# Splitting a bankful of projections over two bursts, and starting a block's projections twelve pairs past its flip

## The chip, the cores and the metric

The kernel runs on one core of one Trainium2 chip. The metric is the device time of one launch in microseconds (us); the median of the runs before is 2676.86 us. The engines are TensorE (PE, with its weight loads listed as PEld), VectorE (DVE), ScalarE (ACT), GpSimd (POOL), and SyncE (SP), which issues most of the DMAs. PE writes its results to PSUM, which has eight banks; one bank holds 128 x 512 float32 values.

## The reference, cut to what matters

Two layers of two kinds alternate, A B A B, over a sequence of S = 2048 tokens with D = 576 features, 32 heads of 18 features each. A is attention with one shared head of keys and values, B is linear attention with a feature map of two softmaxes:

```python
# A: x + A(layernorm(x)); 32 query heads, one key and one value head
q = (x @ wq).reshape(B, S, H, Dh).transpose(0, 2, 1, 3)
k, v = x @ wk, x @ wv
p = softmax(einsum("bhqd,bkd->bhqk", q, k) * Dh ** -0.5)
o = einsum("bhqk,bkd->bhqd", p, v).reshape(B, S, H * Dh) @ wo

# B: x + B(layernorm(x)); linear attention
q, k, v = split(x @ wqkv)
pq, pk = q @ w_phi, k @ w_phi                          # per head
phi = concatenate([softmax(p), softmax(-p)])           # for pq and for pk
kv, z = einsum("bhsf,bhsd->bhfd", phi_k, v), phi_k.sum(s)
o = (phi_q @ kv) / (phi_q @ z + 1e-6) @ wo
```

## The kernel before, in words

The attention of A is the long part of the kernel, a loop that is run once in each of the two A/B layers, in `attend`. It goes over 16 blocks of 128 tokens (`c`), each in two groups of 16 heads (`g`), and for each group over the 16 key tiles (`t`). One (`c`, `g`, `t`, half of the heads) is a *pair*: two score matmuls of 512 columns that run side by side on the two halves of PE's rows (L574), written to one `sc` tile of two banks, and one exponential of 1024 columns on ACT (L1047) that reads `sc` and writes a `pt` tile. There are three `sc` tiles, so the scores of a pair need the exponential three pairs earlier to be done. Two pairs of a key tile make one *value step*: eight matmul records (L853, float32 in two passes) that add probabilities times values to the group's accumulator, one PSUM bank. A layer has 1024 pairs and 512 value steps, and 64 pairs go to one block of tokens.

The six score banks leave two banks. They are called `ps` and `acc`: one of them is the accumulator of the running group, the other is the spare bank for all other PE work. When a group opens (its value step `t == 0`), `homes.reverse()` swaps the two: the spare bank becomes the new accumulator.

The other PE work of the loop is the projections of A's output and of layer B. They run for one block of 128 tokens after the other, as PE has room between scores and values. A *bankful* is one 128 x 288 result: 14 matmuls (L257), because each float32 product is made of a high and a low part. A block of tokens takes eight bankfuls: two of the output projection (weights `wd`, named `wdhi` and `wdlo` in the profile), then two of keys (`wa`), two of values (`wb`) and two of B's queries (`wc`), and then 32 small matmuls that update B's state (L651, the *update*, stored by `kv`). When a bankful is complete DVE copies it out of the spare bank (L607 for keys and queries, L638 for values, L321 for the output). For keys and queries DVE then makes minima, maxima and differences (L609 to L612) and ACT takes an exponential (L614). Ahead of the second query bankful, DVE normalises the first (`feature_end`: L619 to L621).

When a group closes, DVE turns its accumulator (`turned`, L955), divides it by its sums, turns it back (`osb`) and splits it in high and low parts (L134, L135). `tick()` issues the next piece of that work, up to twice in a burst.

The order on PE and on DVE is written by the program and pinned with `in_order()`. `burst()` writes it: three pairs of scores; then a bankful if the `credit`, which grows by the pace of 0.39 in each burst, has reached 1, if the burst before had none and if enough `pt` tiles are free; otherwise two value steps, or three when the next burst will have a bankful, and the update if it is its turn. When the projections have nothing to do (`idle`), the loop goes in steps of two pairs and one value step.

`stream()` decides which projection work comes next. A block that has its attention output added is *flipped*: normalised on DVE and turned through DRAM (`flip_tokens`, `fetch_tokens`), then split in high and low parts on DVE (`turn_tokens`, `split_tokens`), and then its keys, values and queries begin (`mix`) once `wanted()` says so. Before, that is when the attention of the next block has closed, or when fewer than 100 pairs are left.

Of the kernel before, what the change touches and what calls it, by code (L numbers as in the profile page):

```python
# [19 lines left out]
P = 128  # L20
# [4 lines left out]
NT = S // P  # L25
# [3 lines left out]
NG = 2  # L29
# [33 lines left out]
def kernel(ctx, tc, x_in, wq, wk, wv, wo, wqkv, w_phi, wob, out):  # L63
# [264 lines left out]
    def fold_phi(ps, pool, slow, more, folded):  # L328
# [35 lines left out]
        def turn():  # L364
# [12 lines left out]
            for _ in range(2):  # L377
                yield STAGE
# [548 lines left out]
    def attend(layer, st, a1o, stream):  # L927
# [13 lines left out]
        with ctx1:  # L941
# [65 lines left out]
            kind, credit, paused = [None], [0.0], [False]  # L1007
# [12 lines left out]
            def fill():  # L1020
                kind[0] = None
                while True:
                    v = next(bulk[0])
                    assert v is not STAGE
                    if v < 0:
                        break
                in_order()
# [68 lines left out]
            def sums(until):  # L1096
                while done[0] < until:
                    n, t, _ = units[2 * done[0]]
                    values(*groups[n], t, [pts.pop((n, t, hh)) for hh in range(2)])
                    done[0] += 1  # L1100
                    in_order()
# [4 lines left out]
            def burst():  # L1106
# [5 lines left out]
                if work == "P" and credit[0] >= 1 and not paused[0] and held <= TILES:  # L1112
                    fill()
                    credit[0] -= 1
                    paused[0] = True
                else:
                    paused[0] = False
                    count = 3 if credit[0] + st["pace"] >= 1 else 2
                    until = min(ready, max(done[0] + count, -(-(at[0] + BURST - TILES) // 2)))
                    opens = any(t % NT == 0 for t in range(done[0], until))  # L1120
                    if work == "F" and credit[0] >= 1 and not opens:
                        fill()
                        credit[0] -= 1
                        until = min(until, max(done[0] + 1, -(-(at[0] + BURST - TILES) // 2)))
# [23 lines left out]
    BURST = 3  # L1148
    TILES = 9
# [3 lines left out]
    PACES = ((0.6, 0.39), (0.39, 0.39))  # L1153
    FLIP = 84
    TAIL = 100
# [123 lines left out]
    for layer in range(LAYERS):  # L1279
        last = layer == LAYERS - 1  # L1280
        st.update(start_state(bw), added=set(), loaded=set())
        with tc.tile_pool(name="a1o", bufs=2) as a1o:
# [12 lines left out]
            def stream(v, layer=layer):  # L1295
# [58 lines left out]
                settled = 0  # L1354

                def turn_tokens():
                    nonlocal xs, fetched, settled
                    if fetched is not None:
# [4 lines left out]
                def wanted():  # L1363
                    return (xs is not None and xs[0] != KEPT and v.left() <= settled
                            and (xs[0] < st["closed"] or xs[0] == NT - 2 or v.left() < TAIL))

                def flip(i, stats):
                    nonlocal fetched
# [3 lines left out]
                    fetched = i, fetch_tokens(i)  # L1372
# [24 lines left out]
                while v.left():  # L1397
                    if finished:
                        yield from finish_tile()
                    elif turning and xs is None:  # L1400
# [3 lines left out]
                        yield from rest(8)  # L1404
                        turn_tokens()
                    elif fetched is not None and xs is None:
                        yield from rest(8)
                        turn_tokens()
                    elif fetched is None and xs is None and unflipped and v.left() > FLIP:
# [7 lines left out]
                        yield from rest(8)  # L1417
                        turn_tokens()
# [158 lines left out]
```

## Time and profile before

| | |
|---|---|
| runs | 2676.86 us median of 3 (2673.14 to 2677.76) |
| the profiled execution's own time | 2676.42 us |
| its span, first to last instruction | 2674.6 us |
| mean granted TensorE clock | 0.991 of full speed |
| PE busy | 2602.2 us, 97% |
| ACT busy | 2153.8 us, 81% |
| DVE busy | 1265.0 us, 47% |
| ACT idle before the loop's exponentials | 180.4 us, of it 160.3 us waiting for scores |

The loop of the first layer fills the time from about 111 to 1216 us of the span, that of the second from about 1449 to 2525 us. Ahead of, between and behind them lie the first projections of queries, B's read-out and the weights of the next layer, which the change leaves as they are. The ends of matmuls in the profile are modelled, and PE shows as busy nearly everywhere in the loops; how fast the loop runs is better read from the starts of its score matmuls. In the rows below the columns of a timeline are: start in us, length in us, engine, line, operation, result and operands, shapes, number of instructions merged, and in brackets the idle time before it and what ended it.

### The profile page before, as it was taken

The page shows a single profiled execution, that of the slowest core. Times are in us where ns is not written, and L with a number is a line of the kernel's source. Part 1 is how long each engine was busy: PE and PEld are TensorE (multiplying, and loading weights), DVE is VectorE, ACT ScalarE, POOL GpSimd, SP SyncE. Part 2 cuts the span into 40 slices and gives each one's busy share as a digit, 9 for nine tenths or more (in the row PEclk, how much of TensorE's full clock was granted, in tenths as well). Part 3 has the DMA queues.
Part 4 walks back from the last instruction along what each step waited for, and adds up shares of the span by engine and source line. Part 5 has one row for each costly group of instructions (what it writes and reads, how often), then busy time and mean ns, then how long its engine had stood idle before and what let it go on. Part 6 is the DMA issues. An engine that isn't in the chain of part 4 may idle for free. (4 is left out here: it accounts for less than half of the span.)

```text
span 2674.6 us, 55524 instructions
## 1 busy us (share of the span) xinstructions
PE 2602.2 (97%) x22002; PEld 1442.2 (54%) x22002; DVE 1265.0 (47%) x2871; ACT 2153.8 (81%) x2529; POOL 66.0 (2%) x106
## 2 busy tenths in 40 slices
PE   7989999999999999999999999999999999999999
PEld 6633454445444444438996344444444444444498
DVE  8435354444444444436774424444444444444265
ACT  4588889989999999994334999999999999999821
POOL 1000000000000000002000000000000000000010
PEclk9999999999999999999999999999999999999999
DMA  5466243222222222225643312222222222222164
GB/s 182 144 146 171 70 127 100 59 53 60 60 59 57 55 57 57 59 66 158 188 152 105 105 51 59 60 60 60 59 60 59 60 60 57 56 55 55 48 196 140
DMA packets 491634, 232.97 MB, mean 87 GB/s; under 512 B 237734, under 2 KB 458214, under 8 KB 491366
## 3 DMA queue, kind: packets, MB, share of 16 engines
q1 hardware_dynamic: 489894, 226.37, 31.4%
q8 instruction: 177, 2.90, 0.5%
q10 hardware_dynamic: 1472, 2.95, 0.4%
q14 instruction: 91, 0.75, 0.1%
HBM read 130.62 MB, written 96.67 MB: 85 GB/s over the span
## 5 line engine op out<-in xcount | busy, mean ns | idle before, releaser
L1047 ACT ACTIVATE pt<-sc 128x1024 f32<-128x1024 f32 x2036 | 1923.4, 1054 | 180.4 <-PE sc L574 160.3
L574 PE MATMUL sc<-qst,kst 56*128 56x512 f32 x3840 | 698.6, 452 | 21.0 <-ACT pt L1047 20.6
L574 PEld LDWEIGHTS sc<-qst,kst 56*128 56x128 f32 x3840 | 319.4, 185 | 561.7 <-ACT pt L1047 511.8
L853 PE MATMUL acc<-pt,vst 128*32 128x512 f32 x4096 | 499.8, 600 | 0.1
L853 PE MATMUL ps<-pt,vst 128*32 128x512 f32 x4048 | 486.7, 604 | 6.1 <-DVE featq L607 3.2
L853 PEld LDWEIGHTS ps<-pt,vst 128*32 128x32 f32 x4048 | 109.8, 110 | 234.0 <-issue 226.1
L853 PEld LDWEIGHTS acc<-pt,vst 128*32 128x32 f32 x4096 | 104.6, 109 | 211.7 <-issue 209.2
L321 DVE TENSOR_TENSOR xc<-xc,acc 128x288 f32<-128x288 f32 x60 | 27.3, 455 | 349.5 <-PE acc L257 349.5
L257 PE MATMUL ps<-wahi,xs 128*128 128x288 f32 x702 | 152.5, 304 | 2.5 <-ACT xs L132 1.9
L257 PE MATMUL ps<-wchi,xs 128*128 128x288 f32 x576 | 127.2, 307 | 0.0
L257 PE MATMUL acc<-wdhi,on 128*128 128x288 f32 x540 | 120.6, 309 | 3.3 <-DMA on<-od 3.3
L257 PEld LDWEIGHTS ps<-wahi,xs 128*128 128x128 f32 x702 | 116.1, 190 | 7.1 <-ACT xs L132 2.6
L257 PE MATMUL ps<-walo,xs 128*128 128x288 f32 x390 | 114.9, 297 | 0.0
L452 PE MATMUL ps<-xsc,wbhi 128*128 128x256 f32 x576 | 107.3, 285 | 0.6 <-ACT xsc L132 0.6
L474 ACT ACTIVATE pc<-ps 128x256 fp32r<-128x256 f32 x80 | 30.4, 384 | 94.0 <-PE ps L452 92.5
L257 PEld LDWEIGHTS ps<-wchi,xs 128*128 128x128 f32 x576 | 94.1, 188 | 19.0 <-issue 18.1
L607 DVE COPY featk<-acc 128x288 f32<-128x288 f32 x50 | 22.8, 457 | 172.0 <-PE acc L257 172.0
L132 ACT ACTIVATE xs<-ps 128x512 fp32r<-128x512 f32 x36 | 21.4, 595 | 102.6 <-PE ps L307 102.6
L257 PEld LDWEIGHTS acc<-wdhi,on 128*128 128x128 f32 x540 | 88.8, 189 | 25.0 <-issue 23.6
L257 PE MATMUL acc<-wahi,xs 128*128 128x288 f32 x450 | 100.0, 308 | 0.5
L257 PE MATMUL ps<-wclo,xs 128*128 128x288 f32 x320 | 94.3, 295 | 0.0
L452 PEld LDWEIGHTS ps<-xsc,wbhi 128*128 128x128 f32 x576 | 91.2, 192 | 1.6 <-ACT xsc L132 1.1
(261 smaller groups left out, 3062.3 us busy)
## 6 DMA issues: line engine op xcount, KB each, us to landing
qst<-qd SPq DMA_DIRECT2D x360, 72.0 KB
od<-parts SPq DMA_DIRECT2D x512, 36.0 KB
pht<-phi SPq DMA_DIRECT2D x32, 540.0 KB
qd<-pc SPq DMA_DIRECT2D x64, 256.0 KB
on<-od SPq DMA_DIRECT2D x60, 256.0 KB
phi<-pht SPq DMA_DIRECT2D x104, 144.0 KB
xd<-xc SPq DMA_DIRECT2D x33, 288.0 KB
flipped<-pht SPq DMA_DIRECT2D x112, 72.0 KB
```

The costliest lines, as they stand in the source:

```text
L132: A.activation(dst_hi, src, AF.Copy)
L257: T.matmul(dst, xs[:, slot, :], w[half][:, k, c0 : c0 + HALF], start=(n == 0), stop=(n == last))
L321: V.tensor_add(xr, xr, po)
L452: T.matmul(po, lhs, xsc[:, slot, :], start=(n == 0), stop=(n == LASTP))
L474: A.activation(pc[:, 0, :], po, AF.Copy)
L574: T.matmul(sc, kst[head_rows(h), t * P : (t + 1) * P], q[head_rows(h), h // 2, :], start=True, stop=True)
L607: V.tensor_copy(e[:, hs, 0, :], src)
L853: T.matmul(acc[32 * j : 32 * j + 32, :], vst[:, t, :], pts[j], start=first, stop=last)
L1047: A.activation(pt, sc, AF.Exp, scale=SCALE)
```

## The change

Three things are changed in the loop; nothing of what is computed changes.

1. A bankful may be written in two parts. In a burst that follows one without projections, with half a credit, the new branch writes one value step, then the first `PIECE` steps of the bankful (6 of its 14 matmuls); in a later burst it writes one value step and the other 8. Each part takes half a credit. A bankful that can go whole (a full credit, enough free `pt` tiles) still does, as before with no value step beside it. A part is not begun where a group opens within the next six value steps; a group that opens while a bankful is parted has its rest written first. The pace falls from 0.39 to 0.38.
2. `mix` of block `i` may begin when the loop is two pairs short of the end of block `i + 1`, whether that block is closed or not (`BLOCK`, `EARLY`); the rule with `TAIL` goes.
3. The split of a flipped block (`turn_tokens`) waits for `RIPE` = 12 pairs since its flip, instead of eight ticks; finished blocks go first.

In the folding of the weights of the first layer, one load now also waits for a free buffer before it is issued.

```diff
--- before.py
+++ after.py
@@ -375,6 +375,8 @@
                     ready[0] = n - 2
                     yield STAGE
             for _ in range(2):
+                yield STAGE
+            while len(units) - done[0] > len(wts):
                 yield STAGE
             load(len(units) - 1)
             for n in range(2):
@@ -1004,7 +1006,7 @@
                                 tc.add_manual_dep(i, last[PE], SYNC if loads_at[0] is None else NOSYNC, reason="order")
                                 loads_at[0] = i.name
 
-            kind, credit, paused = [None], [0.0], [False]
+            kind, credit, paused, parted = [None], [0.0], [False], [False]
 
             def peek():
                 while kind[0] is None and bulk:
@@ -1017,13 +1019,16 @@
                         kind[0] = v
                 return kind[0]
 
-            def fill():
-                kind[0] = None
-                while True:
+            def fill(steps=None):
+                while steps != 0:
                     v = next(bulk[0])
                     assert v is not STAGE
                     if v < 0:
+                        kind[0], parted[0] = None, False
                         break
+                    if steps is not None:
+                        steps -= 1
+                        parted[0] = True
                 in_order()
 
             last = {}
@@ -1096,6 +1101,8 @@
             def sums(until):
                 while done[0] < until:
                     n, t, _ = units[2 * done[0]]
+                    if t == 0 and parted[0]:
+                        fill()
                     values(*groups[n], t, [pts.pop((n, t, hh)) for hh in range(2)])
                     done[0] += 1
                     in_order()
@@ -1109,19 +1116,28 @@
                 earn(BURST)
                 work = peek()
                 held = at[0] + BURST - 2 * done[0]
-                if work == "P" and credit[0] >= 1 and not paused[0] and held <= TILES:
-                    fill()
-                    credit[0] -= 1
+                forced = -(-(at[0] + BURST - TILES) // 2)
+                opens = any(t % NT == 0 for t in range(done[0], done[0] + 6))
+                whole = credit[0] >= 1 and held <= TILES and not parted[0]
+                if (work == "P" and credit[0] >= (1 if whole else 0.5) and not paused[0]
+                        and held <= TILES + 2 and (whole or parted[0] or not opens)):
+                    if whole:
+                        fill()
+                        credit[0] -= 1
+                    else:
+                        sums(min(ready, max(done[0] + 1, forced)))
+                        fill(None if parted[0] else PIECE)
+                        credit[0] -= 0.5
                     paused[0] = True
                 else:
                     paused[0] = False
                     count = 3 if credit[0] + st["pace"] >= 1 else 2
-                    until = min(ready, max(done[0] + count, -(-(at[0] + BURST - TILES) // 2)))
+                    until = min(ready, max(done[0] + count, forced))
                     opens = any(t % NT == 0 for t in range(done[0], until))
                     if work == "F" and credit[0] >= 1 and not opens:
                         fill()
                         credit[0] -= 1
-                        until = min(until, max(done[0] + 1, -(-(at[0] + BURST - TILES) // 2)))
+                        until = min(until, max(done[0] + 1, forced))
                     sums(until)
                     if work == "U":
                         fill()
@@ -1146,13 +1162,16 @@
                 run(gen)
 
     BURST = 3
+    PIECE = 3
     TILES = 9
     DUE = 9
     SPILL = 4
     SETTLE = 3
-    PACES = ((0.6, 0.39), (0.39, 0.39))
+    PACES = ((0.6, 0.38), (0.38, 0.38))
     FLIP = 84
-    TAIL = 100
+    BLOCK = 2 * NG * NT
+    EARLY = 2
+    RIPE = 12
     KEPT = NT - 3
     PE = mybir.EngineType.PE
     PINNED = (PE, mybir.EngineType.DVE)
@@ -1351,25 +1370,25 @@
                 fetched = xs = None
                 weights = False
 
-                settled = 0
+                settled = ripe = 0
 
                 def turn_tokens():
                     nonlocal xs, fetched, settled
-                    if fetched is not None:
+                    if fetched is not None and v.left() <= ripe:
                         xs = fetched[0], split_tokens(fetched[1])
                         fetched = None
                         settled = v.left() - SETTLE
 
                 def wanted():
-                    return (xs is not None and xs[0] != KEPT and v.left() <= settled
-                            and (xs[0] < st["closed"] or xs[0] == NT - 2 or v.left() < TAIL))
+                    return (xs is not None and xs[0] != KEPT
+                            and v.left() <= min(settled, (NT - 2 - xs[0]) * BLOCK + EARLY))
 
                 def flip(i, stats):
-                    nonlocal fetched
+                    nonlocal fetched, ripe
                     unflipped.remove(i)
                     spoiled.add(i)
                     flip_tokens(i, stats)
-                    fetched = i, fetch_tokens(i)
+                    fetched, ripe = (i, fetch_tokens(i)), v.left() - RIPE
 
                 turning = {}
 
@@ -1401,10 +1420,8 @@
                         while slow:
                             yield from rest(1)
                         turn_next()
-                        yield from rest(8)
-                        turn_tokens()
                     elif fetched is not None and xs is None:
-                        yield from rest(8)
+                        yield from wait(lambda: v.left() > ripe and not finished)
                         turn_tokens()
                     elif fetched is None and xs is None and unflipped and v.left() > FLIP:
                         i = unflipped[0]
@@ -1414,8 +1431,6 @@
                         while slow:
                             yield from rest(1)
                         flip(i, ln_stats([i]))
-                        yield from rest(8)
-                        turn_tokens()
                     elif wanted():
                         if not weights:
                             yield from wait(lambda: not st["loaded"] >= {"wk", "wv"} and v.left())
```

The order of PE shows the parts. At a bankful of the second layer's loop (`wd` and `wc` are weights, `on` and `xs` the tokens; `sc` are scores, `vst` value steps), before it goes whole:

```order
L574 MATMUL sc<-qst,kst 128x512 x6
L257 MATMUL ps<-wchi,xs 128x288
L257 MATMUL ps<-wclo_18357,xs 128x288
L257 MATMUL ps<-wchi,xs 128x288 x2
L257 MATMUL ps<-wclo_18357,xs 128x288
L257 MATMUL ps<-wchi,xs 128x288 x2
L257 MATMUL ps<-wclo_18357,xs 128x288
L257 MATMUL ps<-wchi,xs 128x288 x2
L257 MATMUL ps<-wclo_18358,xs 128x288
L257 MATMUL ps<-wchi,xs 128x288 x2
L257 MATMUL ps<-wclo_18358,xs 128x288
L574 MATMUL sc<-qst,kst 128x512 x6
```

and a parted one, its first part and the burst behind it:

```order
L576 MATMUL sc<-qst,kst 128x512 x6
L855 MATMUL ps<-pt,vst 32x512 x4
L257 MATMUL acc<-wdhi,on 128x288
L257 MATMUL acc<-wdlo,on 128x288
L257 MATMUL acc<-wdhi,on 128x288 x2
L257 MATMUL acc<-wdlo,on 128x288
L257 MATMUL acc<-wdhi,on 128x288
L576 MATMUL sc<-qst,kst 128x512 x6
L855 MATMUL ps<-pt,vst 32x512 x12
```

The bankful of 14 matmuls has become six behind one value step here (`x4` is one step, `x12` are three), and eight behind another two bursts later. Line numbers have moved by two.

With the bankfuls at other places, the openings of groups have other neighbours on PE. In the second layer before, an opening (the change of the value steps from `ps` to `acc`) has value steps around it:

```order
L574 MATMUL sc<-qst,kst 128x512 x6
L853 MATMUL ps<-pt,vst 32x512 x8
L574 MATMUL sc<-qst,kst 128x512 x6
L853 MATMUL acc<-pt,vst 32x512 x8
L574 MATMUL sc<-qst,kst 128x512 x6
L853 MATMUL acc<-pt,vst 32x512 x8
L574 MATMUL sc<-qst,kst 128x512 x6
```

and one in the changed kernel has a whole bankful of queries in the spare bank right before it (its last two rows are shown):

```order
L257 MATMUL ps<-wchi,xs 128x288 x2
L257 MATMUL ps<-wclo_18358,xs 128x288
L576 MATMUL sc<-qst,kst 128x512 x6
L855 MATMUL ps<-pt,vst 32x512 x8
L653 MATMUL acc<-featk,vb_17326 32x36 x32
```

The new group's first value step now writes the bank `ps` that the bankful has just filled, so that it has to come after DVE's copy of it. On DVE, that copy (`featq<-ps`) stands in the changed kernel behind the whole work of the group that has closed and behind the normalising of the first query bankful:

```order
L957 STREAM_TRANSPOSE turned<-acc 128x512
L961 RECIPROCAL rd<-turned 128x16
L962 TENSOR_TENSOR turned<-turned,rd 128x512
L964 STREAM_TRANSPOSE osb<-turned 128x512
L134 CAST parts<-osb 128x512
L135 TENSOR_TENSOR parts<-osb,parts 128x512
L621 TENSOR_REDUCE fz<-featq 128x32
L622 RECIPROCAL fz<-fz 128x32
L623 TENSOR_TENSOR featq<-featq,fz 128x576
L609 COPY featq<-ps 128x16x18
```

At the same opening before, the rows behind the group's own work are copies of key bankfuls that PE writes after the opening:

```order
L955 STREAM_TRANSPOSE turned<-acc 128x512
L959 RECIPROCAL rd<-turned 128x16
L960 TENSOR_TENSOR turned<-turned,rd 128x512
L962 STREAM_TRANSPOSE osb<-turned 128x512
L134 CAST parts<-osb 128x512
L135 TENSOR_TENSOR parts<-osb,parts 128x512
L607 COPY featk<-acc 128x16x18
```

Moved here are the two query bankfuls of a block: from behind the opening's neighbourhood to right before it.

## Prediction

> **What bounds the kernel now.** I began with the page: its engine shares and the two largest groups.
>
> ```profile
> PE 2602.2 (97%) x22002; PEld 1442.2 (54%) x22002; DVE 1265.0 (47%) x2871; ACT 2153.8 (81%) x2529; POOL 66.0 (2%) x106
> L1047 ACT ACTIVATE pt<-sc 128x1024 f32<-128x1024 f32 x2036 | 1923.4, 1054 | 180.4 <-PE sc L574 160.3
> L574 PEld LDWEIGHTS sc<-qst,kst 56*128 56x128 f32 x3840 | 319.4, 185 | 561.7 <-ACT pt L1047 511.8
> ```
>
> ACT waits for scores (160.3 us) and the scores' weight loads wait for ACT (511.8 us): the loop has two limits that take turns. Next, the groups of instructions in a steady stretch of the second layer's loop, 1600 to 2400 us:
>
> ```profile
> L1047 ACT ACTIVATE pt<-sc 128x1024 f32<-128x1024 f32 x750 | 710.7, 1032 | 64.3 <-PE sc L574 55.5
> ```
>
> A pair costs 800 / 750 = 1.067 us, 68.3 us for the 64 pairs of a block; ACT idles 64.3 of 800 us, the upper bound of what better mixing could win (about 5 us a block). To price a burst I read the timeline of PE, from one score start to the next:
>
> ```profile
> 1703.76 1.07 PE L574 MATMUL sc<-qst,kst 56*128 56x512 f32 x6
> ...
> 1708.04 0.97 PE L574 MATMUL sc<-qst,kst 56*128 56x512 f32 x6
> ...
> 1709.94 0.50 PE L574 MATMUL sc<-qst,kst 56*128 56x512 f32 x2
> ...
> 1712.06 0.91 PE L574 MATMUL sc<-qst,kst 56*128 56x512 f32 x4
> ...
> 1713.89 0.91 PE L574 MATMUL sc<-qst,kst 56*128 56x512 f32 x4
> ...
> 1717.50 0.96 PE L574 MATMUL sc<-qst,kst 56*128 56x512 f32 x6
> ...
> 1718.40 0.40 PE L257 MATMUL acc<-wahi,xs 128*128 128x288 f32 x1
> ...
> 1718.63 0.30 PE L257 MATMUL acc<-walo,xs 128*128 128x288 f32 x1
> ...
> 1719.03 0.30 PE L257 MATMUL acc<-walo,xs 128*128 128x288 f32 x1
> ...
> 1720.45 1.06 PE L574 MATMUL sc<-qst,kst 56*128 56x512 f32 x6
> ...
> 1721.44 2.78 PE L853 MATMUL ps<-pt,vst 128*32 128x512 f32 x24
> ...
> 1724.15 0.97 PE L574 MATMUL sc<-qst,kst 56*128 56x512 f32 x6
> ...
> 1747.07 1.06 PE L574 MATMUL sc<-qst,kst 56*128 56x512 f32 x6
> ...
> 1749.91 1.18 PE L574 MATMUL sc<-qst,kst 56*128 56x512 f32 x6
> ...
> 1752.88 1.05 PE L574 MATMUL sc<-qst,kst 56*128 56x512 f32 x6
> ...
> 1755.71 1.18 PE L574 MATMUL sc<-qst,kst 56*128 56x512 f32 x6
> ...
> 1758.88 0.96 PE L574 MATMUL sc<-qst,kst 56*128 56x512 f32 x6
> ...
> 1762.48 0.73 PE L574 MATMUL sc<-qst,kst 56*128 56x512 f32 x4
> ```
>
> Three pairs of scores with a whole bankful cost 1720.45 - 1717.50 = 2.95 us; with three value steps 3.70; with three and the update 4.28; with one 1.90 (from 1708.04). Two pairs with one step cost 1.83 (from 1712.06), the first of them 2.12 (from 1709.94), and the two-step burst that follows such pairs 3.61 (from 1713.89). Other two-step bursts cost 2.84, 2.97 and 2.83, mean 2.88; a bankful behind them 3.17, the three steps behind that 3.60. So every burst costs the larger of PE's own work and about 2.85 us of ACT's, and with three score tiles hardly anything is carried over: three-step bursts are PE's, two-step bursts ACT's. The three-step bursts are also where ACT has time for the projections' own exponentials.
>
> **Part one: the parts of a bankful.** A part stands behind value steps, and the loop before has one such place, at its end:
>
> ```profile
> 1213.95 2.87 PE L853 MATMUL acc<-pt,vst 128*32 128x512 f32 x24
> ...
> 1216.74 0.19 PEld L257 LDWEIGHTS ps<-wahi,xs 128*128 128x128 f32 x1 [0.84 <-issue]
> ```
>
> A step is 3.70 - 2.84 = 0.86, so the three take 2.58 of the 2.79 us, and going over to a bankful costs 0.21. Scores take 0.99 until the values start (1721.44 - 1720.45); three matmuls take 1719.03 - 1718.63 = 0.40, one 0.133; the whole bankful takes 1720.45 - 1718.40 = 2.05, of which 0.18 is more than 14 x 0.133. The first part then costs 0.99 + 0.86 + 0.21 + 6 x 0.133 + 0.18 = 3.04 us, the second 3.31. Lower bound: 2.84 and 2.95, if the transitions vanish under ACT's rhythm; upper: 0.22 more for a first part behind a two-step burst, as for the bankful at 1755.71.
>
> Counted in the orders of both kernels, both loops together: whole bankfuls go from 216 to 166, three-step bursts from 160 to 126, two-step 137 to 180, two-pair 138 to 79, one-step 27 to 6, three steps with update 24 to 19, two with update 2 to 7, and there are 50 first and 50 second parts and one more burst of four pairs with a step (taken as 1.90 + 0.92). The changes by these prices: -50 x 2.95 - 34 x 3.70 + 43 x 2.88 - 59 x 1.83 - 21 x 1.90 - 5 x 4.28 + 5 x 3.46 + 2.8 = -298.6; + 50 x 3.04 + 50 x 3.31 = +317.5; together +18.9. The slow returns from two-pair to two-step bursts go from 27 to 3 (-24 x 0.73 = -17.5), the entries behind a one-step burst from 21 to 1 (-20 x 0.29 = -5.8), and bankfuls or parts right behind a two-step burst from 57 to 116, at 0.22 - 0.10 each (+7.1). **Term 1: +2.7 us**, between -25 and +12. The smoother order is eaten by its own transitions: the stretches of two pairs that it fills were ACT's cheapest.
>
> **Part two: exponentials without cover.** In the second layer before, all 52 exponentials of keys and queries come behind a three-step burst; in the changed order 21 of them, and in the first layer 27 instead of 7, come behind a two-step burst, where ACT has no slack. The first layer shows such a place:
>
> ```profile
> 457.76 1.17 PE L574 MATMUL sc<-qst,kst 56*128 56x512 f32 x6
> 458.25 0.70 ACT L614 ACTIVATE featq<-featq 128x576 f32<-128x576 f32 x1
> ...
> 467.16 1.06 PE L574 MATMUL sc<-qst,kst 56*128 56x512 f32 x6
> ```
>
> Two two-step bursts and a bankful take 467.16 - 457.76 = 9.40 us here, 2.97 + 2.83 + 3.17 = 8.97 without: 0.43. Bounds are 0, if a longer part behind it takes it up, and its own length, 0.70. I take 0.35, a little under the one place seen: **term 2, 41 x 0.35 = +14.4 us** (0 to 29).
>
> **Part three: openings.** The changed order puts a whole bankful with no value step in between right before 17 openings. Its copy on DVE then stands behind the closing group's work, and the new group's first value step waits for it; behind that on PE are queued the other value steps, the update and the next scores, for which ACT waits. In the first layer before there is such a place:
>
> ```profile
> 323.49 0.72 DVE L955 STREAM_TRANSPOSE turned<-acc 128x512 f32<-128x512 f32 x1 [1.44 <-PE acc L853]
> ...
> 326.28 1.07 PE L574 MATMUL sc<-qst,kst 56*128 56x512 f32 x6
> ...
> 327.07 0.45 DVE L134 CAST wstage<-wstage 128x576 fp32r<-128x576 f32 x1
> ...
> 328.23 0.75 DVE L619 TENSOR_REDUCE fz<-featq 128x32 f32<-128x576 f32 x1
> ...
> 330.08 0.45 DVE L607 COPY featq<-ps 128x288 f32<-128x288 f32 x1
> ...
> 330.58 0.16 PEld L853 LDWEIGHTS ps<-pt,vst 128*32 128x32 f32 x8 [3.54 <-DVE featq L607]
> ...
> 335.49 0.97 PE L574 MATMUL sc<-qst,kst 56*128 56x512 f32 x6
> ```
>
> DVE needs 7.04 us from the turning to the end of the copy; without the weight split (1.16), which the steady blocks don't have, 5.88. PE could start values at 326.28 + 0.99 = 327.27; the copy would be done at 329.37. So the second query bankful, which has the normalising ahead of its copy, costs 2.1 us of stall; that is at seven openings (three and four). At the ten others the 1.85 us from 328.23 to 330.08 fall away and 0.3 is left. The burst at 326.28 took 9.21 instead of 4.28 (4.93 lost), and one other opening lost 4.51 (548.12 - 540.73 against 2.88):
>
> ```profile
> 540.73 0.97 PE L574 MATMUL sc<-qst,kst 56*128 56x512 f32 x6
> ...
> 544.54 3.64 PE L853 MATMUL ps<-pt,vst 128*32 128x512 f32 x16 [2.84 <-DVE featk L607]
> ...
> 548.12 1.22 PE L574 MATMUL sc<-qst,kst 56*128 56x512 f32 x4
> ```
>
> Both come to the new prices, -9.4. **Term 3: 14.7 + 3.0 - 9.4 = +8.3 us**; bounds -3 (only 0.3 each) and +28 (4.93 at the seven).
>
> At 326.28 only 3.3 of the 4.93 us are the wait; the rest is a slower PE behind it, and the clock column of the windows shows it (the 0.98 ahead of the last two numbers):
>
> ```profile
> 300.00:400.00 100.00, 95.92 (x821) 47.90 (x819) 49.38 (x97) 87.10 (x94) 0.54 (x1) 0.98 0.40 113
> ```
>
> I take waits of 2.1 us without that loss. The Trainium skill (TensorE: Matmul & The Clock Gate, Part 1: The HAM clock gate) has the clock halve after an idle window of about 3.4 us; by it the seven waits cost nothing more. The trace is less kind: the group at 540.73 lost time beyond a wait of 2.84 us.
>
> **Part four.** A block's first key bankful right behind the update (11 places instead of 3) waits for the new split of tokens on DVE, which follows the update:
>
> ```profile
> 537.21 0.96 PE L574 MATMUL sc<-qst,kst 56*128 56x512 f32 x6
> ...
> 538.92 0.30 PEld L257 LDWEIGHTS ps<-wahi,xs 128*128 128x128 f32 x2 [0.36 <-DVE xs L135]
> ```
>
> The burst takes 540.73 - 537.21 = 3.52, 0.57 over 2.95: **term 4, 8 x 0.55 = +4.4 us**, between 0 and this. RIPE, the load that waits for its buffer and the moved flips issue the same DMAs and DVE work; the 12 pairs (about 12 us) are more than the old eight ticks needed, and nothing in the steady blocks waits on them, so I cost them at nothing (a few us in the first layer's opening if not).
>
> **Sum.** 2.7 + 14.4 + 8.3 + 4.4 = +29.8 us on the profiled execution's 2676.4 us (span 2674.6 and 1.8 around it), 2706 us; it lies 0.4 us from the median of the runs, 2676.9.
>
> **Rivals.** *Cheap parts:* the two parts cost 2.84 and 2.95, and the exponentials hide in the gaps left. For it speaks that PE's modelled busy time can't show what overlaps; against it the wait of 0.84 us at 1216.74. Then 2676.4 - 25 + 8.3 + 4.4 = 2664 us, faster; with the exponentials hidden it decides once two parts cost under about 5.9 us together, 0.45 less than my 6.35. *Even:* terms 2 and 3 come out at half and term 1 at its negative side (-15): 2676 + 11 + 4 - 15 = 2676 us. *Clock loss at the openings:* the waits of 2.1 us slow PE down as the one at 326.28 did, 4.93 - 3.3 = 1.6 us more at seven openings: 2717 us. That the change does nothing is ruled out by the order, which shows 50 parted bankfuls.
>
> **Chances.** My sum 0.5, clock loss 0.18, cheap parts 0.2, even 0.12. A measurement of this kernel can tell about 0.2% (5.4 us) from no change: slower by more 0.68, within it 0.12, faster 0.2. The range goes from 2664 (cheap parts) to 2730 (clock loss, and 0.70 for each exponential); the sum's own range is 2690 to 2720.
>
> **What would show it.** Right: three-step bursts stay at 3.7, the two parts take 3.0 and 3.3 us; ACT's idle time before L1047 grows or stays near 180 us; L853 waits for DVE featq L607 about 2 us each at seven openings and more than 12 us in all; steady blocks take about 69.5 us instead of 68.3. Wrong: the parts take 2.85 and 2.95, blocks take under 68 us, and no value step waits for a copy, because DVE is ahead of the order that I read.

## The result

| kernel | median (us) | ratio to the kernel before, 95% interval |
|---|---|---|
| before | 2675.6 (4 runs) | 1 |
| changed | 2711.4 (2706.9 to 2714.5, 4 runs) | 1.0134 (1.0117 to 1.0150) |

The change makes the kernel 35.8 us slower; the forecast was 2706 us, 30 us slower. The page of the profiled execution of the changed kernel (its span is 2711.7 us, 37.1 more than before) has these answers to the three rows with which the prediction began; the lines moved down by two to five numbers in the file:

```profile
PE 2619.5 (97%) x22002; PEld 1440.1 (53%) x22002; DVE 1259.4 (46%) x2871; ACT 2150.8 (79%) x2529; POOL 66.0 (2%) x106
L1052 ACT ACTIVATE pt<-sc 128x1024 f32<-128x1024 f32 x2036 | 1923.1, 1048 | 210.5 <-PE sc L576 197.2
L576 PEld LDWEIGHTS sc<-qst,kst 56*128 56x128 f32 x3840 | 316.4, 185 | 501.3 <-ACT pt L1052 443.2
```

ACT waits 197.2 us for scores instead of 160.3, and the scores wait less for ACT (443.2 instead of 511.8): the loop moved from ACT's side to PE's. In the steady stretch of the second layer, 1600 to 2400 us, the groups of ACT show 738 pairs where there were 750:

```profile
L1052 ACT ACTIVATE pt<-sc 128x1024 f32<-128x1024 f32 x738 | 699.8, 1030 | 70.9 <-PE sc L576 65.7
```

That is 1.084 us a pair and 69.4 us a block, against 68.3 before. The waits of PE and of its weight loads (line waited for, then us in total, times, the longest) name two causes:

```profile
PE ps L855 <- DVE featq L609: 11.8, 9, 2.1
PE acc L257 <- DMA on<-od: 11.7, 6, 5.0
```

```profile
PEld ps L855 <- DVE featq L609: 14.7, 9, 2.4
PEld ps L257 <- DVE turned L957: 8.8, 11, 1.4
```

The first is the opening that the prediction speaks of. The second, a bankful of the output projection that waits for the heads to come back from memory (`on<-od`), took 3.3 us before, and the prediction put nothing down for it. The third, a bankful right behind an opening that waits until the closed group is turned, is small. Where the loss lies in time is told by the first stretch of the first layer, 110 to 330 us, in the windows of both kernels (PE, PEld, DVE, ACT and POOL busy with their instructions, then the granted clock):

```profile
110.00:330.00 220.00, 202.41 (x1411) 87.04 (x1411) 83.87 (x169) 190.89 (x204) 1.10 (x2) 0.96 0.49 129
```

```profile
110.00:330.00 220.00, 196.70 (x1325) 82.64 (x1329) 76.94 (x155) 177.04 (x190) 1.10 (x2) 0.91 0.49 129
```

In the same 220 us the changed kernel (second row) gets 14 ACT instructions and 86 matmuls less done, at a clock of 0.91 instead of 0.96. By the starts of the exponentials, 64 to a block, the loss of 37.1 us is made of: the first three blocks of the first layer +14.9 us, its other thirteen +3.0 (two stalls of before are gone there), the second layer's loop +15.8, everything outside the loops +3.4.

### The profile page after: what moved, and what is told of

Its sections match the earlier page's. It is cut to its first block, busy times and chain, and to the rows that moved or that the text cites. A ratio compares the mean times of both kernels' runs of the same rounds, so it can differ in the third digit from the quotient of the medians.

```text
span 2711.7 us, 55598 instructions
## 1 busy us (share of the span) xinstructions
PE 2619.5 (97%) x22002; PEld 1440.1 (53%) x22002; DVE 1259.4 (46%) x2871; ACT 2150.8 (79%) x2529; POOL 66.0 (2%) x106
## 3 DMA queue, kind: packets, MB, share of 16 engines
q10 hardware_dynamic: 1472, 2.95, 0.4%
## 5 line engine op out<-in xcount | busy, mean ns | idle before, releaser
L1052 ACT ACTIVATE pt<-sc 128x1024 f32<-128x1024 f32 x2036 | 1923.1, 1048 | 210.5 <-PE sc L576 197.2
L576 PE MATMUL sc<-qst,kst 56*128 56x512 f32 x3840 | 689.2, 447 | 16.9 <-ACT pt L1052 12.6
L576 PEld LDWEIGHTS sc<-qst,kst 56*128 56x128 f32 x3840 | 316.4, 185 | 501.3 <-ACT pt L1052 443.2
L855 PE MATMUL ps<-pt,vst 128*32 128x512 f32 x4048 | 497.9, 606 | 11.8 <-DVE featq L609 11.8
L257 PE MATMUL ps<-wahi,xs 128*128 128x288 f32 x810 | 177.0, 305 | 4.5 <-DVE turned L957 2.6
L257 PEld LDWEIGHTS ps<-wahi,xs 128*128 128x128 f32 x810 | 134.1, 190 | 12.2 <-issue 3.7
L257 PE MATMUL acc<-wdhi,on 128*128 128x288 f32 x540 | 126.0, 313 | 11.8 <-DMA on<-od 11.7
L257 PE MATMUL ps<-walo,xs 128*128 128x288 f32 x450 | 132.7, 297 | 0.0
L257 PE MATMUL ps<-wbhi,xs 128*128 128x288 f32 x567 | 128.4, 308 | 1.2 <-DVE turned L957 1.1
L640 DVE COPY vb<-ps 128x288 f32<-128x288 f32 x51 | 23.3, 457 | 210.0 <-PE ps L257 210.0
L257 PEld LDWEIGHTS acc<-wdhi,on 128*128 128x128 f32 x540 | 89.7, 189 | 55.5 <-issue 44.9
L257 PEld LDWEIGHTS ps<-wbhi,xs 128*128 128x128 f32 x567 | 93.3, 188 | 38.0 <-issue 26.5
L257 PE MATMUL ps<-wchi,xs 128*128 128x288 f32 x468 | 105.6, 308 | 0.0
L257 PE MATMUL ps<-wblo,xs 128*128 128x288 f32 x315 | 92.7, 295 | 0.0
```

What stands on the lines that cost most here:

```text
L257: T.matmul(dst, xs[:, slot, :], w[half][:, k, c0 : c0 + HALF], start=(n == 0), stop=(n == last))
L576: T.matmul(sc, kst[head_rows(h), t * P : (t + 1) * P], q[head_rows(h), h // 2, :], start=True, stop=True)
L640: V.tensor_copy(dst, heads(po))
L855: T.matmul(acc[32 * j : 32 * j + 32, :], vst[:, t, :], pts[j], start=first, stop=last)
L1052: A.activation(pt, sc, AF.Exp, scale=SCALE)
```

## What waits in the first blocks

The timeline of the changed kernel, and below it that of the kernel before, at the first output projection (start, length, engine, line, operation):

```profile
191.98 0.97 PE L576 MATMUL sc<-qst,kst 56*128 56x512 f32 x6
192.03 3.02 SPq L887 DMA_DIRECT2D od<-parts  x8
...
196.01 0.39 SPq L892 DMA_DIRECT2D on<-od  x1
...
198.94 0.58 PE L257 MATMUL acc<-wdhi,on 128*128 128x288 f32 x1 [5.00 <-DMA on<-od]
...
201.75 1.65 PE L576 MATMUL sc<-qst,kst 56*128 56x512 f32 x6
```

```profile
190.18 2.95 SPq L885 DMA_DIRECT2D od<-parts  x8
...
193.24 1.25 PE L574 MATMUL sc<-qst,kst 56*128 56x512 f32 x6
194.03 0.39 SPq L890 DMA_DIRECT2D on<-od  x1
...
196.91 0.37 PE L257 MATMUL acc<-wdhi,on 128*128 128x288 f32 x1 [2.41 <-DMA on<-od]
...
201.23 1.34 PE L574 MATMUL sc<-qst,kst 56*128 56x512 f32 x6
```

The transfers need about the same time in both: from the first write of the heads to the first matmul that reads them 6.9 us (192.03 to 198.94) and 6.7 us (190.18 to 196.91). What differs is where PE stands in its order: a first part may be written where a whole bankful may not, here a burst sooner. It is not the half credit that lets it in. By the kernel's rules the credit has passed 1 in both kernels here (it grows by 0.6 in each burst of this stretch). What holds a whole bankful back is the number of `pt` tiles in use, at most `TILES` = 9 when the next three pairs are counted in. Counted in the traces, 81 pairs and 37 value steps stand on PE when the burst at 191.98 has written its scores, and just as many in the kernel before at 190.49. That makes 81 + 3 - 2 x 37 = 10 tiles: the kernel before writes two value steps instead and its bankful in the next burst, at 193.24, with 9 tiles. A part may begin with `TILES` + 2 = 11, since the value step beside it frees two.

So the burst with its scores at 191.98 starts before the heads are even sent, and takes 9.77 us instead of about 3.1 (the kernel before loses here too: its burst at 193.24 takes 7.99 us). Behind the wait the six score matmuls take 1.65 us instead of 0.97, and the burst at 201.75 takes 4.92 us. The same comes again at 271.94, with 144 pairs, 68 value steps and so 11 tiles, and the credit at its limit of 2 (9.17 us, and 5.35 us for the burst behind it); there the kernel before loses nothing.

## The experiments

All times were taken beside the kernel before; "against before" is the difference of the medians of one set of runs. The terms of the sum are called as in the prediction.

### Whole bankfuls alone, and parts alone

The change has a part that splits bankfuls and a part that says when projections start. The first kernel has only the second:

```diff
-                if (work == "P" and credit[0] >= (1 if whole else 0.5) and not paused[0]
-                        and held <= TILES + 2 and (whole or parted[0] or not opens)):
+                if work == "P" and whole and not paused[0]:
```

> The changed rules for when a block's projections start, but every bankful whole, so no first or second parts. My theory (the parts with their transitions, and the short bursts that come with them, are what costs): by the prices of the prediction this order's bursts sum to 21.6 us less than the kernel before's; 26 exponentials behind two-step bursts (19 more than before) give 6.7, two openings of the second query kind and 13 others minus the 9.4 of before -1.3, eleven more bankfuls right behind an update about 4: 2676 - 12 = 2664 us, faster than before. Rival (the parts are harmless, and the new starting rules for the projections are what costs): near the changed kernel, 2695 to 2711 us.

2683.9 us, 9.6 against before, ratio 1.0030 (1.0019 to 1.0041). Neither number was met. The waits of its weight loads say for the most part why my theory was 20 us too low:

```profile
PEld ps L855 <- DVE featk L609: 10.4, 4, 3.3
...
PEld ps L855 <- DVE featq L609: 5.9, 2, 3.5
```

I had taken 0.3 us for an opening that a key bankful stands before; four of them waited 2.6 us each, and the clock fell behind some of the waits. All fifteen openings together lose 23 us beyond their prices, where 8 were forecast. The splitting still is the larger part of the loss, 26.2 of 35.8 us.

The second kernel keeps parts and pace and goes back to the starting rules of before:

```diff
-                    if fetched is not None and v.left() <= ripe:
+                    if fetched is not None:
...
-                            and v.left() <= min(settled, (NT - 2 - xs[0]) * BLOCK + EARLY))
+                    return (xs is not None and xs[0] != KEPT and v.left() <= settled
+                            and (xs[0] < st["closed"] or xs[0] == NT - 2 or v.left() < TAIL))
```

> Bankfuls in parts and the pace of 0.38, with the old rules for turning tokens and starting projections. My theory: bursts +3.7 us against the kernel before, 42 more exponentials behind two-step bursts 14.7, seven openings of the second query kind and eight others minus 9.4 give 7.7, bankfuls right behind an update 5: 2707 us, as slow as the whole change within 6 us. Rival (the starting rules cost): 2676 to 2685 us.

2708.9 us, 34.6 against before, ratio 1.0133 (1.0112 to 1.0153): my theory. Parts with the old starting rules lose as much as the whole change does.

### The openings

```diff
                     if whole:
+                        if not done[0] % NT:
+                            sums(min(ready, done[0] + 1))
                         fill()
```

> The changed kernel, but where a whole bankful would come right before an opening, the opening value step goes ahead of it in the same burst (17 places); all else keeps its order. My theory (the opening waits for a copy of that bankful, 16 us in the trace of the changed kernel at seven openings, about 3 at the ten others, with half clock after two of them): 14 to 19 us less than the changed kernel, 2692 to 2697 us. Rival (the stall only moves: the bankful now stands right behind the step that opened a group and waits about 1.4 us at 17 places for the closed group's transposition on VectorE, as eleven weight loads of the changed kernel did): 17 x 1.4 = 24 us come back, 2705 us or more.

2700.3 us, 26.0 against before, ratio 1.0091 (1.0078 to 1.0105): 9.8 us less than the changed kernel, between the two expectations. No value step waits for a copy of queries any longer. Seven openings had lost 16.6 us beyond their prices and the ten others 1.4, so some eight come back, part of it at the bankful behind the opening, as the timeline of such a burst shows:

```profile
1690.93 0.99 PE L576 MATMUL sc<-qst,kst 56*128 56x512 f32 x6
1691.07 0.72 DVE L957 STREAM_TRANSPOSE turned<-ps 128x512 f32<-128x512 f32 x1 [5.37 <-PE ps L855]
...
1691.85 1.07 PE L855 MATMUL acc<-pt,vst 128*32 128x512 f32 x8
...
1692.85 0.19 PEld L257 LDWEIGHTS ps<-wdhi,on 128*128 128x128 f32 x1 [0.84 <-DVE turned L962]
...
1694.90 0.97 PE L576 MATMUL sc<-qst,kst 56*128 56x512 f32 x6
```

A burst with the opening step and a whole bankful takes 3.97 us here and 4.13 on the mean of seventeen, where the prices of a step (0.86) and a bankful (2.95) give 3.81. That mean costs 5.4 us for the seventeen; the rest I have not placed. In the profiled executions the second layer's loop is 9.5 us shorter than in the changed kernel, the first layer's no shorter, though three of the seven openings lie there; its waits for the heads grew from 11.7 to 13.9 us.

A harder rule allows no whole bankful at all there. Since the projections then no longer fit, the pace was raised and the last flips allowed later:

```diff
-                whole = credit[0] >= 1 and held <= TILES and not parted[0]
+                whole = credit[0] >= 1 and held <= TILES and not parted[0] and done[0] % NT
...
-    PACES = ((0.6, 0.38), (0.38, 0.38))
-    FLIP = 84
+    PACES = ((0.6, 0.42), (0.42, 0.42))
+    FLIP = 60
```

> The changed kernel, but no whole bankful starts where the next value step opens a group; so that all projections still find room, the pace is 0.42 instead of 0.38 and a flip may start up to 60 units before the end instead of 84. Openings with a bankful right before them: none instead of 17. My theory: openings -19 us, bursts +6 by the prices of the prediction (more three-step and two-pair bursts), nine fewer exponentials behind two-step bursts -3, ten fewer bankfuls right behind an update -3: 2711 - 19 = 2692 us. Rival (openings cost little, since ACT and the score tiles make up for the waits later): 2708 to 2714 us.

2727.0 us, 52.7 against before, ratio 1.0191 (1.0177 to 1.0204): 35 us over my theory, and worse than the change. The waits of PE name a culprit that neither theory had:

```profile
PE acc L257 <- DMA on<-od: 26.5, 11, 5.1
```

The second layer went the theory's way only in part: its loop takes 1087.7 us, 3.9 less than in the changed kernel, where the opening step first had saved 9.5. In the first layer every third block takes 77 us instead of 69, because with the higher pace the output projection is reached before its heads are back. So this run is no test of the openings, but it points at the transfers.

### The wait for the heads

`DUE` is the number of pairs between asking the heads back and letting their projection begin. The base is the kernel with the opening step first.

```diff
-    DUE = 9
+    DUE = 16
...
-    FLIP = 84
+    FLIP = 60
```

> The changed kernel with the opening step ahead of the bankful as before (2700 us), and the output projection of a closed block may begin 16 units after its heads are asked back from memory instead of 9 (a flip may then start 60 units before the end instead of 84). My theory for the time that is left (24 us over the kernel before, 14 of them in the second block of the first layer, where first parts start sooner than a whole bankful could and wait for the heads, on<-od, 10.7 us in three or four waits, with a slower clock behind them): the waits go, 12 to 16 us less, 2684 to 2690 us. Rival (the first layer's opening waits for its queue of transfers anyway and the stall moves to the next bankful): 2697 us or more.

2684.4 us, 11.0 against before, ratio 1.0043 (1.0029 to 1.0056): 15.0 us less, my theory. The windows show where it comes from; in the first stretch the kernel now does as many matmuls as the kernel before (1417, 1411):

```profile
110.00:330.00 220.00, 202.52 (x1417) 84.48 (x1418) 81.48 (x165) 189.46 (x203) 1.10 (x2) 0.95 0.50 132
```

By the starts of the exponentials its first three blocks take 210.1 us, against 223.9 in the changed kernel and 209.0 before. No wait for `on<-od` is left there. One of 7.2 us for the folding of the weights stands in the list in its place:

```profile
PE acc L257 <- DVE featk L411: 7.2, 1, 7.2
```

The kernel before had 3.4 us of this wait at another bankful (DVE featk L409), the changed one 5.5: part of the stall did move, but most of it went. Both constants were changed at once; what `FLIP` does alone was not run.

### Whole bankfuls with the two repairs

```diff
-                if (work == "P" and credit[0] >= (1 if whole else 0.5) and not paused[0]
-                        and held <= TILES + 2 and (whole or parted[0] or not opens)):
+                if work == "P" and whole and not paused[0]:
                     if whole:
+                        if not done[0] % NT:
+                            sums(min(ready, done[0] + 1))
                         fill()
```

> Whole bankfuls only (2684 us), and the opening step ahead of a bankful that would come right before it (15 places). My theory: its six waits of value steps for a copy, 16.3 us at the weight loads, go with the slower clock behind some of them, and about 0.25 us at each of the 15 places comes back: 2666 to 2671 us, faster than the kernel before by 0.2 to 0.3%. Rival (the whole-bankful order itself is no better than that of before; ACT takes the time back): 2676 to 2682 us.

2670.6 us, 2.8 below before, ratio 0.9991 (0.9982 to 1.0000): inside my range in us, though it can't be told from no change.

With `DUE = 16` and `FLIP = 60` as well:

> Whole bankfuls, the opening step first, and the output projections held back to 16 units. My theory: against the same without the holding back some 4 us less (the waits for the heads were 4.9 us in all there), 2662 to 2668 us. Rival (nothing to be had, since a whole bankful starts late enough): within 2 us of it.

2661.7 us, 11.7 below before, ratio 0.9957 (0.9943 to 0.9970), just under the range of my theory. The holding back is worth 8.9 us here too, more than the 5.6 us that PE waits for the heads without it; so not all of the 15.0 us above is peculiar to the parts. This kernel and the one of the section on the heads differ only in the parts: 2684.4 against 2661.7. So **the parts, with all that they bring along, cost 22.7 us** when no value step waits for a copy at an opening and no projection for the heads. Some of it is still stall and not price: the wait of 7.2 us for the folding is 2.5 us here, and the first three blocks take 203.3 us here against 210.1 with parts. The groups of ACT in the stretch from 1600 to 2400 us:

```profile
L1052 ACT ACTIVATE pt<-sc 128x1024 f32<-128x1024 f32 x745 | 704.8, 1035 | 74.3 <-PE sc L576 70.3
```

```profile
L1052 ACT ACTIVATE pt<-sc 128x1024 f32<-128x1024 f32 x751 | 711.3, 1029 | 62.9 <-PE sc L576 55.6
```

With parts (the first) ACT waits 70.3 us for scores, with whole bankfuls 55.6, as before the change (55.5).

### The exponentials

In both kernels the exponentials of keys and queries inside the loops were left out:

```diff
-        A.activation(flat, flat, AF.Exp)
+        if copies is not V:
+            A.activation(flat, flat, AF.Exp)
```

> The kernel before without the exponentials of keys and queries inside both loops (their activations are left out, so the features stay unexponentiated); the order of all else is the same. Each of the 104 is 0.70 us of ACT. My theory: here 97 of them stand behind three-step bursts and are hidden, 7 cost 0.35 each, and two stalls at openings (the copies' chain is 0.7 us shorter) ease a little: 0 to 6 us less, 2668 to 2674 us. Rival (ACT's total work counts, wherever it stands): 104 x 0.35 = 36 us less.

2669.4 us, 3.0 below before, ratio 0.9987 (0.9978 to 0.9996): my theory. Where 97 of 104 stand behind three-step bursts, taking away 73 us of ACT's work is worth 3 us.

> The changed kernel without the same exponentials. My theory (term 2 of the prediction): 48 stand behind two-step bursts and cost 0.35 each: 17 us less, and up to 5 more where the openings' chains are shorter; so its distance to the kernel before shrinks from 36 to about 20 us when both are without. Rival (a longer part or burst behind takes them up, the lower bound of term 2): the distance stays at 32 to 38 us.

2700.2 us, 27.8 against before, ratio 1.0104 (1.0088 to 1.0119). Without the exponentials the distance between the kernels is 30.8 us (2700.2 - 2669.4), with them 35.8. It shrinks by 5.0, not by 14.4 to 16: nearer the rival than my theory, and with intervals of some 4 us on each distance I can't tell it from nothing. At the openings nothing got shorter (the wait is for the copy, which comes ahead of the exponential):

```profile
PEld ps L856 <- DVE featq L609: 17.1, 9, 2.4
```

Seven such openings lose 19.8 us here against 16.6 with the exponentials, because the clock falls at four of them instead of two; without that the distance would have shrunk by some 8 us. An uncovered exponential then costs about 5.0 / 41 = 0.12 us, or 0.2 with the clock allowed for: well below the 0.35 that I took.

### What the starting rules are worth, and a last trial

The two repairs on the kernel before, with its own starting rules and pace:

```diff
                 if work == "P" and credit[0] >= 1 and not paused[0] and held <= TILES:
+                    if not done[0] % NT:
+                        sums(min(ready, done[0] + 1))
                     fill()
...
-    DUE = 9
+    DUE = 16
...
-    FLIP = 84
+    FLIP = 60
```

> The kernel before (its own starting rules, pace 0.39, whole bankfuls) with the two repairs alone: the opening step ahead of a bankful, and output projections held back to 16 units (flips to 60). It tells what the changed starting rules are worth without parts. Theory (nothing: the second layer's loop takes 1075 us with either rules, 1075.8 before and 1075.0 in the whole-bankful order with the two repairs): the first layer loses its two opening stalls, 9.4 us, and some 4 us of waits for the heads: 2659 to 2665 us, as fast as that order's 2662. Rival (the smoother start of projections is worth the 21 us by which its bursts sum to less): 2668 us or more.

2660.6 us, 11.8 below before, ratio 0.9954 (0.9941 to 0.9967): my theory. It is as fast as whole bankfuls with the changed starting rules (2661.7). So these rules win nothing, although by the prices of the prediction, applied to the bursts of both traces, their order sums to about 16 us less. Nine more places with a bankful right behind an update and 20 more uncovered exponentials would take back 4.5 + 2.4 us; nine or ten remain, which is how far such a sum of burst prices can be trusted. In the steady stretch the kernel before with the repairs does 749 pairs in 800 us, where it did 750 and the other rules 751:

```profile
L1047 ACT ACTIVATE pt<-sc 128x1024 f32<-128x1024 f32 x749 | 710.0, 1031 | 62.7 <-PE sc L574 54.1
```

Last, the whole-bankful kernel with both repairs and no bankful right behind an update:

```diff
                     if work == "U":
                         fill()
+                        paused[0] = True
```

> Whole bankfuls, the opening step first, 16 units, and no bankful right behind an update (12 places there). Theory (such a bankful costs 0.5 us more than elsewhere, as the traces show at 3.47 against 2.95, and this order has nine fewer exponentials behind two-step bursts, at 0.1 to 0.2 each): 6 + 1.5 us less, 2653 to 2657 us. Rival (the bankful that comes a burst later pushes the block's projections and other waits take it back): 2659 us or more.

2661.9 us, 10.5 below before, ratio 0.9955 (0.9942 to 0.9969): the rival. Avoiding twelve bursts at 0.5 us gained nothing. In its profile the second layer's first block is 3.5 us longer (63.8 against 60.3), which accounts for part of it in that execution; what takes the rest back is open.

## Why the prediction was right, and where it was not

The time, the sign and the cause in the main, a loop that leaves ACT waiting for scores, came out. Put in order by the runs: the opening step first takes 9.8 us off the changed kernel and holding the heads back 15.0, together 24.8. The same two repairs take 11.8 us off the kernel before, so what the change added at the openings and at the heads is 24.8 - 11.8 = 13.0 us. The other 22.8 us stay between the two repaired kernels (11.0 + 11.8), and 13.0 + 22.8 = 35.8. Of these 22.8, terms 1, 2 and 4 explain 12.1 at most (2.7 and 4.4 as forecast, 5.0 as measured); some ten us are not placed, part of which may be the longer wait for the folding.

**Term 1, the burst prices (+2.7).** The timeline of the changed kernel in a steady stretch has both parts, each from its scores to the next:

```profile
1755.91 1.17 PE L576 MATMUL sc<-qst,kst 56*128 56x512 f32 x6
...
1758.99 0.97 PE L576 MATMUL sc<-qst,kst 56*128 56x512 f32 x6
...
1762.61 0.97 PE L576 MATMUL sc<-qst,kst 56*128 56x512 f32 x6
...
1765.76 0.97 PE L576 MATMUL sc<-qst,kst 56*128 56x512 f32 x6
```

The first part takes 1758.99 - 1755.91 = 3.08, the second 1765.76 - 1762.61 = 3.15, the three steps between them 3.62; the prediction had 3.04, 3.31 and 3.70. In the second layer the means are 3.11 and 3.18. So two parts cost 6.29 us, and not the 5.9 at which the rival *cheap parts* would have decided. The prices of the parts were right; whether the term's sign was can't be told, since the sum is good to ten us only.

**Term 2, exponentials without cover (+14.4): mis-sized.** It measures 5.0 us, 0.12 each (some 8 us with the clock allowed for), and can't be told from nothing. The one place from which I took 0.43 was not typical; the lower bound, that a longer part behind takes them up, is nearer.

**Term 3, the openings (+8.3).** The seven openings behind a second query bankful lose 16.6 us beyond their prices, where 14.7 were forecast, and the ten others 1.4 instead of 3.0; the waits stand in the list as foretold. Five cost 1.78 to 2.09 us and two cost 3.50 and 3.78, because the clock fell there: the rival *clock loss* is true at two places of seven. Taking these places away gave 9.8 us back and not 18.0, in part because the bankful behind an opening waits as well. (The lower bound of this term is -4.3 by its own working, 17 x 0.3 - 9.4, and not -3.)

**Term 4, bankfuls behind an update (+4.4).** Ten of the twelve bursts that the trace shows (the prediction counted eleven) take 3.47 or 3.48 us, 0.52 over 2.95, as forecast; but avoiding them in another order won nothing, so as a term of the time it is not borne out.

**The step that failed** is "RIPE, the load that waits for its buffer and the moved flips ... I cost them at nothing (a few us in the first layer's opening if not)". The place was named, the cause was not. The first three blocks of the first layer lost 14.9 us, and it is the parts that send PE to the output projection before its heads are back, because a first part may begin with two more `pt` tiles in use than a whole bankful. Whole bankfuls with all the edits named there took 206.4 us for these blocks, against 223.9 in the change and 209.0 before; parts with the old starting rules took 221.1. Holding the projections back won 15.0 us, and none of my rivals had it. I had asked of each new burst what it costs, and not what it now reads earlier. That the sum came out within 6 us is in part luck: term 2 was some 9 us too large and the first blocks were 14.9 us short, two errors that cancel in part.

The forecast of 69.5 us for a steady block (69.4 measured), of three-step bursts that stay at 3.7 (3.69 on the mean in the second layer) and of ACT's idle time (210.5 after 180.4) held.

## What to carry to other kernels

A finer grain of filler work does not only cost its transitions: it lets work start sooner, and whatever it reads must be there sooner too, so for every piece that moves forward, look up when its inputs land. Of a new rule, ask which of its conditions in fact lets the work in earlier: here it was the tiles and not the credit that the change names. Stalls that a schedule has at group boundaries are repaired more cheaply at the boundary (one step ahead of the filler, a later due time: 11.8 us here) than by another grain or another pace. And sums of burst prices read from one schedule are good to about ten us in 2670 for another one; a difference smaller than that needs a run.

## What the runs showed that I had not expected

The clock falls after some waits and not after others of the same length. Here are the first value step of two openings of the changed kernel, in the timeline, and the windows of 8 us around them:

```profile
2014.86 4.48 PE L855 MATMUL ps<-pt,vst 128*32 128x512 f32 x24 [1.46 <-DVE featq L609]
...
2435.70 2.78 PE L855 MATMUL ps<-pt,vst 128*32 128x512 f32 x24 [1.46 <-DVE featq L609]
```

```profile
2012.00:2020.00 8.00, 6.43 (x97) 2.44 (x98) 4.52 (x10) 4.27 (x5) 0.00 (x0) 0.79 0.41 109
...
2432.00:2440.00 8.00, 6.38 (x108) 3.15 (x107) 6.12 (x14) 5.53 (x7) 0.00 (x0) 1.00 0.34 88
```

Both waited 1.46 us, with the same work ahead and behind. After the one the same 24 matmuls took 4.48 us, with a mean clock of 0.79 over the window, after the other 2.78 us, with 1.00. Without the exponentials four of the seven openings lost their clock, with them two. A mean of 0.79 over 8 us is half speed for 3.4 us (0.21 x 8 x 2). The Trainium skill (TensorE: Matmul & The Clock Gate, Part 1: The HAM clock gate) has the clock halve after an idle window of about 3.4 us and calls that window free-running. The length of the loss agrees with it; the cause does not, since a wait of 1.46 us cannot fill such a window. That the place of a wait in a free-running window decides would fit the two rows, but no run here shows it.
